# An attention-plus-FFN kernel: attention held to an even rate, shorter output descriptors, wider margins and a new account of DMA times in the scheduler

## Chip, cores, metric

The kernel runs on one core of one Trainium2 chip. The metric is device time in microseconds (us), the median of several executions. Ratios are computed as the mean time of one kernel's fast runs over that of the other kernel's fast runs of the same rounds, so they are not quite the ratio of the medians quoted beside them. Every set of runs has its own runs of the kernel before, made on the same chip.

## The reference, cut to what matters

```python
B, H, S, D = 8, 12, 448, 64            # batch, heads, rows, head size
scores = q @ k^T / 8                    # per head
scores = einsum('bhij,hg->bgij', scores, w_pre)    # heads are mixed before the softmax
attn   = softmax(scores)
attn   = einsum('bhij,hg->bgij', attn, w_post)     # and mixed again after it
x      = (attn @ v), heads side by side # 3584 rows of 768
out    = relu(x @ w_in)**2 @ w_out      # w_in 768x2048, w_out 2048x768, float32 out
```

## The kernel before

The kernel plans its own order. A list scheduler in the program builds one static sequence of instructions for each engine, with a rough account of how long each takes; the order is fixed when the program is built. TensorE has eight streams of units: transposes (T), QK, pre-mix, post-mix, AV, the two halves of the FFN (F1, F2), and a direct form of the first ten pre-mix chunks.

A *chunk* is 10 query rows x 12 heads = 120 partitions; there are 360 chunks. QK scores go from PSUM to an SBUF tile `stage`; a DMA then re-lays each chunk from "one row per partition" to "row and head per partition" (`dring`), so that a matmul can mix heads (pre-mix). ScalarE (ACT) takes the exponential and its row sum, VectorE (DVE) the reciprocal, GpSimd (POOL) folds it into the post-mix weights (`wk2s`), and TensorE mixes again (post-mix).

This is how the scheduler picks the next unit for TensorE:

```python
MARGIN = 250.0
MARGIN_DMA = 3000.0
...
    est = max([t.end + SEM_LAT ... for t in needs ...])     # when the inputs should be there
    safe = est + (MARGIN_DMA if u.dma else MARGIN)          # u.dma: the pre-mix, which needs dring
...
    first = min(f[0] for f in found)
    sure = [f for f in found if f[1] <= first + 1.0]        # those that are ready with the margin
    if sure:
        late = self.ahead()
        def rank(f):
            p = u.prio                                      # post 2, pre 3, QK 4, ... F1 6, F2 7
            if late and u.paced:                            # pre-mix and post-mix are paced
                p += 5.0
            ...
        f = min(sure, key=rank)
    else:
        f = min(found, key=lambda f: (f[0], f[2].prio))     # nothing is sure: the earliest
```

With `ahead()` true, FFN units go before pre-mix and post-mix, if FFN units are ready:

```python
        def ahead():
            done = (f_all[0] - len(s_F1)) / f_all[0] + (f_all[1] - len(s_F2)) / f_all[1]
            return NG - len(s_post) > LEAD + NG * done / 2          # LEAD = 60, NG = 360
```

So before, attention could run up to 60 chunks ahead of the FFN's share of the work. The scheduler also keeps an account of DMA times (a re-layout "move" takes 480 ns of service, more behind loads). The output rows leave like this (`osb` is the SBUF tile that they leave from):

```python
        osb = sb("osb", [128, NOS, F], DT.float32)                  # F = 768
        ...
        dst = bass.AP(out.tensor, row * F, [[RJ * F, m], [1, F]])   # rows of 3072 bytes
        eng.dma_start(dst, osb[p0:p0 + m, s, :]).then_inc(sem_out[s].handle, 16)
```

The softmax here doesn't subtract the row's maximum and nothing guards it: scores larger than these inputs give would overflow.

## Time and profile before

| | before |
|---|---|
| time, median of 3 | 609.08 us (608.08 to 609.39) |
| span of the profiled run | 609.5 us |
| TensorE busy | 582.5 us, 96% |
| mean granted TensorE clock | 0.991 |

The page of the kernel before: busy time of the engines, and TensorE's busy share and granted clock in 40 slices of 15 us, in tenths:

```profile
PE 582.5 (96%) x5998; PEld 391.9 (64%) x5998; DVE 350.3 (57%) x891; ACT 452.2 (74%) x1166; POOL 338.7 (56%) x686
PE   4989999999999899899999999999999999999995
PEclk9989999999999999999899999999999999999998
```

TensorE bounds the kernel: besides the 96%, the page gives it 80% of the chain of work that ended last. But 96% does not say how much is left: in the timeline, 384-column matmuls start every 162 ns, while the page gives 328 ns for one of them. So I measured steps from one matmul's start to the next. For each kind of step I took the usual length, and I call what a step has above it a *wait*, if it is more than 150 ns. (A fixed 0.2 us at the row-tiled QK pairs is left out.) In the profile of before this gives 22.6 us of waits in a stream of 594 us: 7.6 in the first 80 us, 1.5 from 80 to 160, 4.3 from 160 to 240, 6.9 from 240 to 320 and 2.3 afterwards. (The level depends on what is taken as usual. A recount of all the traces, made when this text was checked, takes the median for each pair of successive kinds of matmul, so that the longer step at a change of tiling mode does not count as a wait: in before, a post-mix matmul is followed by the next post-mix after 52 ns, by a QK matmul after 145 (medians). It gives 19.7 us here and 12.4 after the change; sizes differ by a microsecond or a few, and the directions named in this text hold in both counts unless it says otherwise.)

The view of waits of before, TensorE alone (total us, times, longest):

```profile
PE ps L577 <- DMA kraw<-in_k_dram: 8.1, 1, 8.1
PE ps L776 <- DMA dring<-stage: 4.3, 7, 1.0
PE ps L840 <- POOL wk2s L810: 1.6, 3, 0.7
PE ps L701 <- ACT stage L377: 1.3, 3, 0.9
PE ps L840 <- ACT stage L377: 0.9, 3, 0.4
```

The first line is the start (the first load of k), which the orders hardly change: 8.1 to 8.8 us in before, after, e1, e2, e5, e7 and p1. After that, the pre-mix waits for its re-layout (`dring`, 4.3 us), and QK and post-mix for PSUM banks that evictions of scores (`stage`, 1.3 and 0.9 us) hold. The number of pre-mix matmuls in equal stretches of before (the windows view of tile `dring`; the count after x is what to read):

```profile
80.00:160.00 80.00, 19.56 (x60) 7.62 (x60) 1.00 0.82 149
160.00:240.00 80.00, 19.30 (x60) 7.27 (x59) 1.00 0.79 148
240.00:320.00 80.00, 19.43 (x61) 7.80 (x61) 0.98 0.72 131
320.00:400.00 80.00, 11.98 (x45) 5.68 (x45) 1.00 0.54 106
400.00:480.00 80.00, 9.41 (x41) 5.37 (x41) 1.00 0.44 85
```

Attention is done at 60 chunks per 80 us up to 320 us and at 41 to 45 afterwards. The stretch with many chunks is where the waits are.

The timeline of TensorE before, around 292 us (start, length, instructions, and in brackets the idle time ahead of them):

```profile
291.59 0.39 PE L701 MATMUL ps<-qkt 64*88 64x448 bf16 x2
292.83 0.91 PE L701 MATMUL ps<-qkt 64*88 64x448 bf16 x4 [0.86 <-ACT stage L377]
293.88 0.38 PE L840 MATMUL ps<-wk2s,pring 120*128 120x120 bf16 x4
294.10 0.35 PE L776 MATMUL ps<-dring,wk 120*120 120x448 bf16 x1
294.68 0.58 PE L840 MATMUL ps<-wk2s,pring 120*128 120x120 bf16 x4 [0.23 <-ACT stage L377]
295.06 2.77 PE L1043 MATMUL ps<-w_out_sb,h2t 128*128 128x384 bf16 x8
```

After about two microseconds of waits, eight 384-column matmuls take 2.77 us, twice what they take elsewhere (8 x 162 ns = 1.3 us). The record of the granted clock has an interval of 3.413 us at 0.5 from 294.6 us on.

### The profile page before, as it was taken

The page shows a single profiled execution, that of the slowest core. Times are in us where ns is not written, and L with a number is a line of the kernel's source. Part 1 is how long each engine was busy: PE and PEld are TensorE (multiplying, and loading weights), DVE is VectorE, ACT ScalarE, POOL GpSimd, SP SyncE. Part 2 cuts the span into 40 slices and gives each one's busy share as a digit, 9 for nine tenths or more (in the row PEclk, how much of TensorE's full clock was granted, in tenths as well). Part 3 has the DMA queues.
Part 4 walks back from the last instruction along what each step waited for, and adds up shares of the span by engine and source line. Part 5 has one row for each costly group of instructions (what it writes and reads, how often), then busy time and mean ns, then how long its engine had stood idle before and what let it go on. Part 6 is the DMA issues. An engine that isn't in the chain of part 4 may idle for free.

```text
span 609.5 us, 15842 instructions
## 1 busy us (share of the span) xinstructions
PE 582.5 (96%) x5998; PEld 391.9 (64%) x5998; DVE 350.3 (57%) x891; ACT 452.2 (74%) x1166; POOL 338.7 (56%) x686
## 2 busy tenths in 40 slices
PE   4989999999999899899999999999999999999995
PEld 3657776677776556566565666657655765566963
DVE  4777876688778568747674355643544365432410
ACT  1887848888979698889797788787788786665621
POOL 8688586295946366755367543466357444842011
PEclk9989999999999999999899999999999999999998
DMA  9999879686978785768586274525642386311002
GB/s 138 180 225 210 136 125 184 144 147 127 165 134 151 148 176 98 121 111 148 127 152 114 48 153 103 125 47 84 142 102 46 71 151 147 63 21 53 27 29 76
DMA packets 94762, 72.38 MB, mean 119 GB/s; under 512 B 6160, under 2 KB 92640, under 8 KB 94688
## 3 DMA queue, kind: packets, MB, share of 16 engines
q0 software_dynamic: 48992, 33.83, 35.8%
q1 hardware_dynamic: 45696, 37.56, 28.6%
q8 instruction: 48, 0.79, 0.5%
q14 instruction: 26, 0.21, 0.1%
HBM read 45.70 MB, written 11.01 MB: 93 GB/s over the span
## 4 chain that ended last, share of the span: by engine, by line
PE 80%; DMA 8%; ACT 4%; SPq 3%; DVE 2%; POOL 1%; issue 1%; POOLq 0%; ACTq 0%; DVEq 0%
PE ps L1043 23%; PE ps L961 20%; PE ps L840 11%; PE ps L776 10%; DMA dring<-stage 7%; PE ps L902 7%; PE ps L701 6%; PE ps L577 3%; SPq L748 3%; ACT stage L377 2%; DMA kraw<-in_k_dram 1%; ACT pring L794 1%; DVE w_out_sb L621 1%; POOL h2t L999 1%; DVE stage L378 1%
## 5 line engine op out<-in xcount | busy, mean ns | idle before, releaser
L794 ACT ACTIVATE pring<-ps 120x448 bf16<-120x448 f32 x360 | 192.0, 553 | 28.2 <-PE ps L776 26.8
L810 POOL TENSOR_SCALAR wk2s<-wk2b,rinv 120x120 bf16<-120x120 bf16 x350 | 124.9, 364 | 114.1 <-DVE rinv L804 111.5
L961 PE MATMUL ps<-xt,w_in_sb 128*128 128x448 bf16 (+6 forms) x1248 | 171.6, 281 | 1.1 <-issue 0.5
L1043 PE MATMUL ps<-w_out_sb,h2t 128*128 128x384 bf16 x896 | 170.3, 328 | 0.1
L378 DVE CAST a2t<-ps 112x480 bf16<-112x480 f32 x205 | 131.3, 651 | 57.4 <-PE ps L840 55.0
L999 POOL TENSOR_TENSOR h2t<-h1t 128x448 bf16<-128x448 bf16 (+6 forms) x176 | 113.5, 659 | 42.0 <-ACT h1t L989 21.7
L961 PEld LDWEIGHTS ps<-xt,w_in_sb 128*128 128x128 bf16 x1248 | 99.7, 98 | 46.3 <-issue 7.3
L840 PE MATMUL ps<-wk2s,pring 120*128 120x120 bf16 x1440 | 120.8, 217 | 3.5 <-POOL wk2s L810 1.6
L840 PEld LDWEIGHTS ps<-wk2s,pring 120*128 120x128 bf16 x1440 | 94.7, 98 | 44.7 <-issue 5.7
L1043 PEld LDWEIGHTS ps<-w_out_sb,h2t 128*128 128x128 bf16 x896 | 83.9, 98 | 52.9 <-issue 5.0
L378 DVE CAST stage<-ps 120x896 bf16<-120x896 f32 (+2 forms) x87 | 93.6, 1083 | 31.3 <-PE ps L701 20.6
L776 PE MATMUL ps<-dring,wk 120*120 120x448 bf16 x350 | 103.1, 357 | 4.9 <-DMA dring<-stage 4.3
L377 ACT ACTIVATE stage<-ps 120x896 bf16<-120x896 f32 (+3 forms) x99 | 89.1, 917 | 18.3 <-PE ps L701 13.4
L804 DVE RECIPROCAL rinv<-rowsum 120x1 f32<-120x1 f32 x360 | 53.6, 156 | 83.9 <-ACT pring L794 83.0
L377 ACT ACTIVATE a2t<-ps 112x480 bf16<-112x480 f32 x155 | 86.3, 574 | 19.5 <-PE ps L840 17.3
L794 ACT ACTIVATION_READ_ACCUMULATOR pring<-ps 120x1 f32 x360 | 78.2, 217 | 0.0
L1089 POOL DMA_DIRECT2D out_dram<-osb x56 | 30.7, 549 | 68.4 <-ACT osb L377 60.7
L989 ACT ACTIVATE h1t<-ps 128x448 bf16<-128x448 f32 (+5 forms) x105 | 44.6, 429 | 27.7 <-PE ps L961 26.7
L701 PE MATMUL ps<-qkt 64*120 64x448 bf16 (+3 forms) x372 | 58.3, 378 | 2.1 <-ACT stage L377 1.3
L776 PEld LDWEIGHTS ps<-dring,wk 120*120 120x120 bf16 x350 | 44.2, 133 | 21.2 <-DMA dring<-stage 3.7
L990 DVE TENSOR_SCALAR h1t<-ps 128x448 bf16<-128x448 f32 (+6 forms) x103 | 41.6, 407 | 23.4 <-PE ps L961 18.5
L902 PE MATMUL ps<-a2t,vraw 112*64 112x230 bf16 (+5 forms) x864 | 41.1, 255 | 0.0
(37 smaller groups left out, 329.3 us busy)
## 6 DMA issues: line engine op xcount, KB each, us to landing
dring<-stage SPq DMA_DIRECT2D x342, 105.0 KB
vraw<-in_v_dram POOLq DMA_DIRECT2D x24, 224.0 KB, 5.8
qraw<-in_q_dram POOLq DMA_DIRECT2D x23, 224.0 KB, 5.9
kraw<-in_k_dram POOLq DMA_DIRECT2D x23, 224.0 KB, 7.3
w_in_sb<-in_moe_w_in_dram POOLq DMA_DIRECT2D x8, 384.0 KB, 10.4
w_out_sb<-in_moe_w_out_dram POOLq DMA_DIRECT2D x12, 256.0 KB, 33.6
out_dram<-osb POOLq DMA_DIRECT2D x8, 336.0 KB, 3.9
out_dram<-osb POOLq DMA_DIRECT2D x8, 288.0 KB, 3.4
```

Of the source, the lines that this page charges most:

```text
L377: return eng.activation(o, i_, AF.Copy)
L378: return eng.tensor_copy(o, i_)
L701: r_ = eng.matmul(ps[0:nr, banks[par], 0:S], qkt[r0:r0 + 64, pb, p, 0, i0:i1], qkt[r0:r0 + 64, pb, p, 1, :], start=True, stop=True,)
L776: return eng.matmul(ps[0:NR, bank, 0:S], wk1[:, :, :], dring[:, slot, :], start=True, stop=True)
L794: return eng.activation(pring[:, pr, 0:S], ps[0:NR, bank, 0:S], AF.Exp, accum_out=rowsum[:, pr, :])
L804: return eng.reciprocal(rinv[:, pr, :], rowsum[:, pr, :])
L810: return eng.tensor_scalar(wk2s[:, ws, :], wk2b[:, :, :].rearrange("p a b -> p (a b)"), rinv[:, pr, :], 1.0, op0=ALU.mult, op1=ALU.mult)
L840: r_ = eng.matmul(ps[0:128, bank, jb * NR:(jb + 1) * NR], pring[:, pr, jb * JB:jb * JB + 128], wk2s[:, ws, :], start=True, stop=True,)
L902: r_ = eng.matmul(ps[kk * 64:kk * 64 + 64, bank, x * n:(x + 1) * n], vraw[:, h, r, :], a2t[half][:, r, h, a0:a0 + n], start=(r == 0), stop ...
L961: r_ = eng.matmul(ps[:, bank, 0:n], w_in_sb[:, ft, t16 * 128:(t16 + 1) * 128], xt[:, ft, c0:c1], start=(ft == 0), stop=(ft == NFT - 1),)
L999: return eng.tensor_tensor(h2t[:, t16, o0:o0 + n], h1t[:, s, 0:n], h1t[:, s, 0:n], ALU.mult)
L1043: r_ = eng.matmul(ps[:, bank, 0:FH], h2t[:, t16, col:col + 128], w_out_sb[:, t16, hh * FH:(hh + 1) * FH], start=(t16 == 0), stop=(t16 == N ...
```

## The change

Its intent: spread attention evenly, so that neither the re-layout DMA nor the evictions are crowded; put consumers further behind producers; and keep large output packets out of the way of re-layout packets. The diff, cut to its core:

```diff
-MARGIN = 250.0
-MARGIN_DMA = 3000.0
+MARGIN = 500
+MARGIN_DMA = 4000
 ...                                   # the scheduler's account of a move behind loads
-                    at += min(behind, 2600.0)
-                    service += 600.0
+                    at += min(behind, 2000.0)
+                    service += min(behind, 12.0 * max(
+                        [45.0] + [x.dma[2] for x in self.loads if x.end > at]))
 ...
-                t.end = self.move_free + 2100.0
+                t.end = self.move_free + 2200.0
 ...
-        LEAD = 60
+        LEAD = 70
+        PACE = (60000, 30, 1400)
+        OP = F // 4
 ...
-        osb = sb("osb", [128, NOS, F], DT.float32)
+        osb = sb("osb", [128, NOS, 4, OP + 8], DT.float32)
 ...                                   # a move's service 480 -> 620
-                        dst = bass.AP(out.tensor, row * F, [[RJ * F, m], [1, F]])
+                        dst = bass.AP(out.tensor, row * F, [[RJ * F, m], [OP, 4], [1, OP]])
 ...                                   # an output's service n * 350 -> n * 200 + 1000
-            return NG - len(s_post) > LEAD + NG * done / 2
+            made = NG - len(s_post)
+            return made > LEAD + NG * done / 2 or made > PACE[1] + (
+                plan.free[PE] - PACE[0]) / PACE[2]
```

So there are four parts: the *pace* (one chunk per 1.4 us while FFN is ready), the *margins*, the *DMA account* of the scheduler (which the short description of the change does not name) and the *short rows* (768-byte pieces). The first three move only the order of instructions; no matmul is added or removed.

More of the change, by code (lines that the diff above doesn't have):

```diff
@@ L129, in _commit @@
         if t.dma:
-            kind, service = t.dma
+            kind, service, piece = t.dma
             if kind == "load":
@@ L488, in put @@
                                      after=[last.get("load")],
-                                     dma=("load", step * S * D * 4 * LOADR))
+                                     dma=("load", step * S * D * 4 * LOADR, 45.0))
                         last["load"] = t
@@ L514, in put @@
                         -2e5 + VPOS if b == 0 else b * 1000.0 - 1600.0, sem_v, 16,
-                        dma=("load", 4 * S * D * 4 * LOADR)))
+                        dma=("load", 4 * S * D * 4 * LOADR, 45.0)))
                     if len(ts) == 3:
@@ L546, in emit_load_w @@
                         (-2e5 if i == 0 and j == 0 else WPRIO + i) + j * 0.1, sem_w[i][j], 16,
-                        after=[last.get("load")], dma=("load", F * FF // NWP // nx * 4 * LOAD))
+                        after=[last.get("load")], dma=("load", F * FF // NWP // nx * 4 * LOAD, 45.0))
                     last["load"] = t
@@ L752, in emit_rel @@
             t = plan.add("rel%d_%d" % (b, c), SP, fn, sev[(b, T)] + [pre_of.get(g - NDS) if g - NDS >= ND else None],
-                         {SP: (815.0, 0.0)}, g * 1.0, sem_dsl[slot], 16, dma=("move", 480.0))
+                         {SP: (815.0, 0.0)}, g * 1.0, sem_dsl[slot], 16, dma=("move", 620.0, 0.0))
             rel[g] = t
@@ L1064, in fn_oe @@
             def fn_oe(eng, en, hh=hh, bank=bank, s=s):
-                return copy(eng, en, osb[:, s, hh * FH:(hh + 1) * FH], ps[:, bank, 0:FH])
+                return copy(eng, en, osb[:, s, 2 * hh:2 * hh + 2, 0:OP],
+                            ps[:, bank, 0:FH].rearrange("p (a b) -> p a b", a=2))
             t_oe = add("oev%d_%d_%d" % (b, tile, hh), FLEX, fn_oe, [t_o, o_free.get(s)],
@@ L1087, in fn_od @@
                     for p0, m, row in pieces:
-                        dst = bass.AP(out.tensor, row * F, [[RJ * F, m], [1, F]])
-                        eng.dma_start(dst, osb[p0:p0 + m, s, :]).then_inc(
+                        dst = bass.AP(out.tensor, row * F, [[RJ * F, m], [OP, 4], [1, OP]])
+                        eng.dma_start(dst, osb[p0:p0 + m, s, :, 0:OP]).then_inc(
                             sem_out[s].handle, 16)
@@ L1095, in after_F2 @@
                                 {POOL: (580.0 * n, 0.0)}, b * 1000.0 + 710,
-                                sem_out[s], 16 * n, dma=("load", n * 350.0))
+                                sem_out[s], 16 * n, dma=("load", n * 200.0 + 1000.0, 45.0))
                 o_free[s] = t_od
```

## The prediction

> **What bounds the kernel now.** TensorE. The page gives it 582.5 of 609.5 us busy (96%); the chain of waits is 80% PE. I took start-to-start steps from the timeline: 448-column matmuls follow each other every 189 ns, 384-column ones every 162, 120-column ones every 52. All PE instructions at those rates sum to about 560 us. With 8.1 us before the first transpose (wait for kraw) and about 7 us from the last matmul to the end, some 575 us is a floor (estimate from the trace); about 34 us are mode changes beyond that sum, clock dips and waits.

> Waits over 150 ns in the PE stream (without the fixed 0.2 us at each row-tiled QK pair, line 701) add up to only about 20 us: 5 us in the first 40 us, 13 us from 40 to 330, 2 us after. By releaser: DMA dring<-stage about 6 us (8 waits, worst at 193-203 and 245-252 us), evictions of QK scores (stage) about 7, GpSimd's wk2s folds 2, clock dips 1 to 3.

> **What the change does.** (1) The pace rule holds attention at one chunk per 1.4 us while FFN is ready. From the order of instructions: before, chunks come at 17 to 18 per 20 us of PE work from 160 to 280 us, then stop and go; after, 14 to 15 from 120 to 360. (2) Margins 250 to 500 and 3000 to 4000 ns put consumers further behind producers; runs of the pre-mix matmul (line 776) fall from 212 to 141, PE groups from 996 to 893. No matmul is removed; I count 14 more mode changes at about 0.1 us: +1.3 us. ([...] the trace shows 280 instead of 186 ns at such a step.) (3) An output packet of 6144 B takes 239 ns on a DMA engine, one of 3072 B 121, an 896-byte dring packet 54; [...]. With 768 B a dring packet would wait about 50 ns (estimate from 512- and 896-byte packets) instead of up to 239. But outputs are in flight only in 28 short bursts: worth 0 to 2 us. GpSimd issues get dearer: now 541 ns; loads with four pieces per row take about 740, so +0.2 us x 56 = 11 us on an engine 56% busy, and perhaps +0.5 us at the tail.

> **Critical path.** At most the 15 us of waits after 40 us can go; I expect 9 to 10 of them to go, less 1.3 us of mode changes and 0.5 us of tail: about -7.5 us.

> **Prediction:** 601.5 us, 8 in 10 between 596.5 and 608.5. Faster by over 2%: 0.12; same: 0.85; slower: 0.03.

> **What would show it.** PE waits for dring below 2 us; waits for stage evictions halved; PE waits between 160 and 320 us at the level of 330 to 480; output packets of 768 B near 50 ns; output issues near 730 ns; last matmul about 7 us earlier; the same 8 us at the start.

> **What would make it wrong.** New waits where pre-mix matmuls come in batches (ACT needs 770 ns for each exponential), long output landings that hold osb, more half-clock intervals, a gap at the end of the attention; the other way, evictions that unblock more than I count.

## The result

| | before | after |
|---|---|---|
| median | 609.24 us (608.08 to 609.68, 4 runs) | 603.97 us (602.95 to 604.73, 4 runs) |
| ratio of fast runs | | 0.9915 (0.9895 to 0.9936) |
| span, profiled run | 609.5 us | 602.4 us |
| granted clock, profiled run | 0.991 | 0.997 |

The same lines of the page of after:

```profile
PE 579.5 (96%) x5998; PEld 390.1 (65%) x5998; DVE 355.4 (59%) x904; ACT 445.5 (74%) x1153; POOL 341.7 (57%) x686
PE   4988899999999999999999999999999999999995
PEclk9999999999999999999999999999999999999998
```

TensorE's busy share is again 96%: by that number nothing happened. The slices are what changed: from the sixth on there is no 8 left, and the two slices with a lower clock ahead of the last one are gone. The waits of TensorE after (lines of the program have moved by 3):

```profile
PE ps L580 <- DMA kraw<-in_k_dram: 8.4, 1, 8.4
PE ps L843 <- POOL wk2s L813: 2.0, 4, 0.6
PE ps L580 <- issue: 1.0, 1, 1.0
PE ps L779 <- DMA dring<-stage: 0.7, 2, 0.5
PE ps L843 <- DVE h1t L993: 0.5, 1, 0.5
```

The wait for the re-layout fell from 4.3 to 0.7 us. The pre-mix matmuls of after in the same stretches:

```profile
80.00:160.00 80.00, 16.05 (x56) 7.04 (x56) 1.00 0.75 139
160.00:240.00 80.00, 13.96 (x56) 6.93 (x56) 1.00 0.78 144
240.00:320.00 80.00, 13.59 (x55) 6.91 (x55) 1.00 0.68 128
320.00:400.00 80.00, 14.54 (x60) 7.68 (x60) 1.00 0.62 117
400.00:480.00 80.00, 12.75 (x49) 6.13 (x49) 1.00 0.51 99
```

The rate is 55 to 60 up to 400 us, where it was 60 and then 45. By my measure the waits were 22.6 us before and are 16.6 after: 11.2 in the first 80 us (more than the 7.6 of before), 2.6 from 80 to 160, and 2.7 in all the rest, where before had 13.5. From the first to the last matmul, the two profiled runs account as follows:

| | before | after | difference |
|---|---|---|---|
| waits outside half-clock intervals | 21.4 us | 16.6 us | -4.8 |
| lost in half-clock intervals (2, none) | 4.2 us | 0.0 us | -4.2 |
| all else (mode changes 248, 262) | 568.7 us | 570.1 us | +1.4 |
| first to last matmul | 594.3 us | 586.7 us | -7.6 |

The profiled pair differs by more than the medians do (7.1 us of span against 5.3). The profiled run of before was one of the longer of its kind: it took 611.25 us and its clock was 0.991. And of the 4.2 us at most 3.4 can be the clock itself (half of 2 x 3.413 us); the rest is waiting inside the two intervals. In the three sets of experiments below, the runs of before (11 in each) have mean clocks of 0.996, 0.996 and 0.994, while after has 0.997. One 3.413 us interval at half clock costs 0.5 x 3.413 / 608 = 0.0028 of the mean clock, so those runs had on average up to about one such interval more than after (an estimate from these records), and not two. That is why only part of the 4.2 us appears in the medians.

### The profile page after: what moved, and what is told of

Read it like the earlier page. It is cut to its first block, busy times and chain, and to the rows that moved or that the text cites. A ratio compares the mean times of both kernels' runs of the same rounds, so it can differ in the third digit from the quotient of the medians.

```text
span 602.4 us, 15913 instructions
## 1 busy us (share of the span) xinstructions
PE 579.5 (96%) x5998; PEld 390.1 (65%) x5998; DVE 355.4 (59%) x904; ACT 445.5 (74%) x1153; POOL 341.7 (57%) x686
## 4 chain that ended last, share of the span: by engine, by line
PE 89%; DMA 3%; ACT 3%; POOL 2%; SPq 1%; DVE 1%; issue 1%; POOLq 0%
PE ps L1046 25%; PE ps L964 24%; PE ps L843 12%; PE ps L779 10%; PE ps L704 7%; PE ps L905 6%; PE ps L580 4%; DMA dring<-stage 2%; ACT stage L380 1%; SPq L751 1%; DMA kraw<-in_k_dram 1%; POOL h2t L1002 1%; POOL wk2s L813 1%; ACT pring L797 0%; PE ps L653 0%
## 5 line engine op out<-in xcount | busy, mean ns | idle before, releaser
L1046 PE MATMUL ps<-w_out_sb,h2t 128*128 128x384 bf16 x896 | 165.8, 326 | 0.2
L843 PE MATMUL ps<-wk2s,pring 120*128 120x120 bf16 x1440 | 118.0, 216 | 3.3 <-POOL wk2s L813 2.0
L843 PEld LDWEIGHTS ps<-wk2s,pring 120*128 120x128 bf16 x1440 | 92.8, 97 | 43.2 <-issue 7.7
L380 ACT ACTIVATE stage<-ps 120x896 bf16<-120x896 f32 (+3 forms) x104 | 92.9, 919 | 19.2 <-PE ps L704 18.3
L381 DVE CAST stage<-ps 120x896 bf16<-120x896 f32 (+2 forms) x82 | 88.3, 1085 | 19.7 <-PE ps L704 18.8
L779 PE MATMUL ps<-dring,wk 120*120 120x448 bf16 x350 | 90.2, 354 | 1.5 <-DMA dring<-stage 0.7
L1093 POOL DMA_DIRECT2D out_dram<-osb x56 | 35.3, 632 | 76.7 <-ACT osb L380 69.5
L993 DVE TENSOR_SCALAR h1t<-ps 128x448 bf16<-128x448 f32 (+6 forms) x111 | 45.5, 410 | 33.8 <-PE ps L964 28.1
L992 ACT ACTIVATE h1t<-ps 128x448 bf16<-128x448 f32 (+6 forms) x97 | 41.7, 432 | 25.1 <-PE ps L964 23.9
L380 ACT ACTIVATE osb<-ps 128x384 f32<-128x384 f32 x33 | 16.2, 490 | 35.4 <-PE ps L1046 34.9
```

The lines of the kernel that those rows point to most:

```text
L380: return eng.activation(o, i_, AF.Copy)
L381: return eng.tensor_copy(o, i_)
L779: return eng.matmul(ps[0:NR, bank, 0:S], wk1[:, :, :], dring[:, slot, :], start=True, stop=True)
L843: r_ = eng.matmul(ps[0:128, bank, jb * NR:(jb + 1) * NR], pring[:, pr, jb * JB:jb * JB + 128], wk2s[:, ws, :], start=True, stop=True,)
L993: return eng.tensor_scalar(h1t[:, s, 0:n], ps[:, bank, 0:n], 0.0, None, op0=ALU.max)
L1046: r_ = eng.matmul(ps[:, bank, 0:FH], h2t[:, t16, col:col + 128], w_out_sb[:, t16, hh * FH:(hh + 1) * FH], start=(t16 == 0), stop=(t16 == N ...
```

## The experiments

My theory was that the order saves, and that it does so by the pace: fewer chunks per time give the re-layout and the evictions time. The rivals were that the short rows save (re-layout packets pass sooner), that the margins save, or that the DMA account does. Twelve kernels ran, all with five rounds, and all gave correct results.

### The short rows alone, and everything but the short rows

```diff
 # shortened: the copy from PSUM into the padded osb, which goes with it, is left out
 # e1_desc_only: the kernel before with these alone (same order on every engine as before)
+        osb = sb("osb", [128, NOS, 4, OP + 8], DT.float32)
+        dst = bass.AP(out.tensor, row * F, [[RJ * F, m], [OP, 4], [1, OP]])
 # e2_after_long_desc: the kernel after without them (same order on every engine as after)
```

> The kernel before with the 768-byte output rows alone; the order of instructions on every engine is that of before. Schedule theory (the gain comes from the order, the descriptors are worth nothing): 609 us, ratio 1.000 +- 0.002. Descriptor theory (re-layout packets no longer wait behind 6144-byte output packets): about 2 to 5 us less, 604 to 607, and PE waits for dring down by half. Clock theory (each longer PE wait is followed by a 3.4 us interval at half clock, as twice in the before profile, none in the after profile): the clock stays near 0.991 if the waits at 36 and 292 us stay.

> The changed kernel with 3072-byte output rows again; the order of instructions on every engine is that of after. Schedule theory: 604 us, ratio 0.991 to 0.992, clock 0.997, output issues back at 541 ns. Descriptor theory: 606 to 609.

Measured: e1 611.29 us against 609.86 (one of its six runs, 618.54 us at a clock of 0.988, was in the slow state and is not in the ratio), ratio 1.0024 (0.998 to 1.0068). e2 603.83 us, ratio 0.9904 (0.9873 to 0.9935), as good as the whole change. So the short rows are worth nothing that five rounds can show; the gain is in the order. The records of the DMA packets fit this. In before, from rows of 3072 B, output packets have 6144 B (1536 of them, median 239 ns on their DMA engine) or 3072 B (121 ns). In after I had expected 768 B near 50 ns. They have 4608 B (2048 of them, 187 ns), 3072 B (121 ns) or 1536 B (65 ns): six, four or two times the 768 B of a piece, and none has 768 B. By these lengths a re-layout packet that waits for one output packet gains about 50 ns and not 190; that is an estimate from the medians, and that it does wait for one was not shown. The issue on GpSimd did get dearer; the group of before, then that of after:

```profile
L1089 POOL DMA_DIRECT2D out_dram<-osb x56 | 30.7, 549 | 68.4 <-ACT osb L377 60.7 <-DVE rinv L804 5.5 <-issue 1.1
```

```profile
L1093 POOL DMA_DIRECT2D out_dram<-osb x56 | 35.3, 632 | 76.7 <-ACT osb L380 69.5 <-DVE rinv L807 5.9 <-DVE osb L381 0.8
```

That is 549 to 632 ns, 4.6 us in all on an engine that does not bound (busy for 56 and 57% of the span).

e1 also shows how much one order varies between runs. Its order is that of before, and its profile has this in the waits view, where before has 4.3 us:

```profile
PE ps L777 <- DMA dring<-stage: 7.4, 11, 1.3
```

The same goes for the order of after: e2 has it too, and where after has 0.7 us, its profile has

```profile
PE ps L779 <- DMA dring<-stage: 2.4, 5, 0.6
```

Waits for a DMA differ from run to run (e1 and e2 also have the other kind of rows). The fall is in both pairs of profiles, 4.3 to 0.7 and 7.4 to 2.4, but no single figure is firm. The runs of before spread over 606.2 to 612.6 us in this set, those of e2 over 602.7 to 604.2.

### Taking the three scheduler parts apart

```diff
 # in words, not as they stand in the files
 # e5_pace_only, on before:   + PACE = (60000, 30, 1400), LEAD = 70, the new ahead()
 # e3_margins_only, on before: + MARGIN = 500, MARGIN_DMA = 4000
 # e7_model_only, on before:  + the new account of DMA times (short rows not)
 # e8_pace_margins, on before: + pace and margins
 # e4_after_old_margins, on after: - MARGIN = 500, 4000   + 250, 3000
 # e6_after_no_pace, on after:     - PACE, LEAD = 70       + LEAD = 60, the old ahead()
```

> The changed kernel with the old rule of when attention is ahead (LEAD 60, no PACE), everything else as after. If the even pace is what saves: 608 to 610, with PE waits of 13 us or so between 40 and 330 us as before, and dring waits back. If the margins and the cost model save: 603 to 605.

> The changed kernel with the old margins (250 and 3000 ns), everything else as after. If the margins save by putting consumers later: 606 to 609, with more short waits of 0.2 to 0.5 us on stage and dring. If the pace alone saves: 603 to 605, the same waits as after.

> The kernel before with the wider margins alone (500 and 4000 ns). Margin theory: 604 to 606, dring waits below 2 us. Pace theory: 607 to 610. Cost-model theory (the order is only good when the scheduler's account of DMA times is right): 607 to 610.

> The kernel before with the pace rule alone (PACE and LEAD 70), old margins and old DMA account. Pace theory: 604 to 606, and the waits between 160 and 320 us gone while those before 80 us stay. Margin theory: 607 to 610.

> Only the edits to the scheduler's account of DMA times (service 620 for 480 ns, delay behind loads, 200n+1000 for an output), without pace, margins and short rows. Cost-model theory: 604 to 606, dring waits below 2 us. Pace and margin theories: 608 to 610.

> The kernel before with pace and margins, without the new DMA account and the short rows. If the two named edits of the schedule are the whole change: 603 to 605. If the new DMA account matters: 606 to 608 with dring waits of 3 us or more left.

Measured, with the 95% interval. (e4, e6 and after have the short rows, which by e1 and e2 do not matter.) The last three columns are from the profile of each: waits from 80 us on, waits of the pre-mix for `dring` in the whole run, and half-clock intervals of 3.4 us between 50 and 590 us.

| pace | margins | DMA account | kernel | median us | ratio to before | waits after 80 us | dring | half-clock |
|---|---|---|---|---|---|---|---|---|
| - | - | - | before | 609.9, 611.2, 611.4 in three sets | 1 | 15.0 | 5.8 | 1 |
| - | yes | - | e3 | 620.96 | 1.0172 (1.0133 to 1.0211) | 20.4 | 9.1 | 3 |
| - | - | yes | e7 | 624.49 | 1.0239 (1.0189 to 1.029) | 26.3 | 14.9 | 4 |
| - | yes | yes | e6 | 616.94 | 1.0116 (1.0071 to 1.016) | 22.8 | 2.7 | 2 |
| yes | - | - | e5 | 608.42 | 0.997 (0.993 to 1.001) | 12.9 | 1.4 | 0 |
| yes | yes | - | e8 | 610.32 | 1.0009 (0.9964 to 1.0054) | 11.4 | 3.4 | 0 |
| yes | - | yes | e4 | 609.36 | 1.0002 (0.9968 to 1.0037) | 15.2 | 1.2 | 0 |
| yes | yes | yes | after | 603.97 | 0.9915 (0.9895 to 0.9936) | 5.3 | 1.2 | 0 |

No theory that names one part survives as I had put it. Pace alone gives 0.3%, not the whole. Margins alone make it 1.7% slower and the DMA account alone 2.4%. e8 and e4 are no better than before, although each lacks only one part. Yet the pace is ahead in every pair that differs by it alone: 1 against 0.997, 1.0172 against 1.0009, 1.0239 against 1.0002, 1.0116 against 0.9915. The first of these differences is within the noise (the interval of e5 reaches 1.001); the other three are not. In the profiles the last column splits the same way: no half-clock interval after 50 us in the orders with the pace, one to four in those without it. But that is one profile of each kernel. The mean clock of all fast runs, which includes the time before 50 us, is 0.996 for e5, for e8 and for before in the same set, so between these three the split does not show; it shows for e3 (0.992), e6 (0.990) and e7 (0.982). In the recount of waits, e5, e8 and e4 have less from 80 us on than before (9.0, 7.8 and 10.6 us against 12.4) and still no shorter time beyond the noise: the waits after 80 us alone do not set the time. The extreme is e7, whose waits view and clock line of the page read:

```profile
PE ps L779 <- DMA dring<-stage: 11.7, 16, 1.4
```

```profile
PEclk9999999997999999999799999999999999999998
```

### Is the order a draw?

That every single edit of the scheduler other than the pace made before slower was suspicious. A list scheduler is chaotic: a small edit gives another order. If before had been tuned until a good order came out, then any edit loses that order, and the loss is put down to the edit. So I nudged both kernels by values that mean nothing.

```diff
 # n2_before_margin260:  - MARGIN = 250.0   + MARGIN = 260.0
 # n1_after_margin520:   - MARGIN = 500     + MARGIN = 520
```

> The kernel before with MARGIN 260 instead of 250, again a nudge without meaning. If before was itself tuned to a lucky draw (which would explain that single edits to it cost 1.7 and 2.4%): 612 to 625. If its rules are worth 610: 607 to 613.

> The changed kernel with MARGIN 520 instead of 500, a nudge that has no meaning of its own but gives another order (PE groups 900 instead of 893). If the gain belongs to the rules: 602 to 606. If the order is a draw of which the changed kernel got a good one: anywhere from 602 to 612.

Measured: n2 619.18 us against 611.36, ratio 1.0124 (1.0077 to 1.0172); one of its six runs, the profiled one, 626.23 us at a clock of 0.983, was in the slow state and is not in the ratio. n1 605.17 us, ratio 0.9916 (0.9876 to 0.9955). So ten nanoseconds of margin cost before 1.2%, and twenty cost after nothing. The order of before looks like a lucky one of its rules; that of after did not prove so under the one nudge that it was given. Over the five orders without pace (before, n2, e3, e7, e6) the mean ratio is (1 + 1.0124 + 1.0172 + 1.0239 + 1.0116) / 5 = 1.013, and before is the best of them. Over the six with pace (e5, e8, e4, after, n1, and v1 below) it is (0.997 + 1.0009 + 1.0002 + 0.9915 + 0.9916 + 0.9931) / 6 = 0.996. By that estimate the pace is worth about 1.7%; the four pairs above, alike in the other scheduler parts, give 1.6% on average. Most of it does not show when before and after are compared, because before is 1.3% better than the mean of its five. It stays an estimate: each order is one draw, and the orders of a group differ in the other parts too.

What this leaves open: whether margins and DMA account are worth the 0.9% by which e8 and e4 trail after. Each of them is one order, and the order of one kernel moved by 1.2% under a nudge. Two good neighbours (after and n1) speak for it; they do not settle it.

### The early waits of after

After has more waits in its first 80 us than before. The pace line allows 16 chunks at 40 us, 30 at 60 and 44 at 80. In the trace of after, 18, 28 and 45 post-mixes have started by then, so the rule is at its limit in this stretch and may be what makes the waits.

```diff
 # v1_early_off, on after
-            return made > LEAD + NG * done / 2 or made > PACE[1] + (
-                plan.free[PE] - PACE[0]) / PACE[2]
+            return made > LEAD + NG * done / 2 or (
+                plan.free[PE] > 80000 and made > PACE[1] + (plan.free[PE] - PACE[0]) / PACE[2])
```

> The changed kernel with the pace rule off for the first 80 us, where the changed kernel has 11.2 us of PE waits against 7.6 before. If the rule causes those early waits: about 8 us of them and 600 to 602 us. If the early waits come with the latency of the first chunks whatever the rule: 603 to 607.

Measured: 606.37 us, ratio 0.9931 (0.9893 to 0.9969). I had expected 600 to 602 us if the rule causes the early waits. The early waits did fall, to 7.0 us (one profile), so the rule does seem to cause 4 us of them; but those from 80 to 160 us rose from 2.6 to 6.6 and the sum is 20.0 against 16.6. That the chunks which are not held back early are crowded a little later is my reading of this; it was not tested. As an improvement this fails, and no version that I ran beats after by more than the noise.

### What a wait costs

```diff
 # p1_five_stalls, on after, when the order is made (shortened, partly in words)
+        for at in (150e3, 220e3, 290e3, 360e3, 430e3):
+            x = <the first F1 task on TensorE that ends after `at`>; y = <the next one on TensorE>
+            <SP: once x is done, load 128 x 12 values to a scratch tile>; y waits for that load
```

> The changed kernel with TensorE made to wait five times, at about 150, 220, 290, 360 and 430 us, for a small load issued when the instruction before was done. Each wait should be 2.5 to 3.5 us. If waits only cost themselves: 604 + 5 x 3 = about 619 us and a clock of 0.997. If a wait of 2 us or more within one 3.41 us interval brings an interval at half clock: some of the five also show one, the clock falls to 0.985 or so, and each costs about 1.7 us more: 622 to 628.

Measured: 637.5 us, ratio 1.0424 (1.0378 to 1.047), clock 0.97 in the profiled run. I had expected waits of 3 us; two were longer (4.9 and 9.9): there the small load was issued late, behind re-layouts on its queue, and in the longer one it also took 8.1 us to land, beside loads of q and k. The sum of the five idle times is 2.8 + 9.9 + 4.9 + 2.6 + 3.0 = 23.2 us, but the profiled span grew by 638.9 - 602.4 = 36.5 us. The rest, 13.3 us, goes with ten half-clock intervals of 3.413 us. (Half of their time is 17 us, but in some of it TensorE was waiting anyway.) Each of the five waits has one or more of them, from 160.4, 238.9, 320.8, 402.8 and 477.9 us on, starting within the wait or right after it, and after 50 us there are no others; the one at 37.5 us was not made by them and followed other waits. The profile of after has none. The first of the five in the timeline:

```profile
158.12 0.45 PE L964 MATMUL ps<-xt,w_in_sb 128*128 128x218 bf16 x3
161.35 0.63 PE L704 MATMUL ps<-qkt 64*120 64x448 bf16 x2 [2.77 <-DMA scratch<-in_w_pre_dram]
161.91 0.73 PE L964 MATMUL ps<-xt,w_in_sb 128*128 128x218 bf16 x3
162.43 2.45 PE L779 MATMUL ps<-dring,wk 120*120 120x448 bf16 x6
```

After 2.77 us of idle time, six pre-mix matmuls take 2.45 us, where at full clock one starts every 189 ns. And its page:

```profile
PEclk9989999999799997999979999899999999999998
```

So each of these five waits, of 2.6 to 9.9 us, brought the half clock, and not the reverse; for shorter waits in pieces only the correlation is shown. In an ordinary run a smaller share of the gain of after comes this way than in the profiled pair, as said above: the clock of before was 0.994 to 0.996 on average, and 0.997 in after.

## Why the prediction was right

The time was 603.97 us, inside 596.5 to 608.5, and "same" (within 2%) was the class with 0.85. Point by point:

- **"TensorE is nearly dense; at most 15 us of waits after 40 us can go."** Right, and it is what kept the forecast small. Waits from 80 us on fell from 15.0 to 5.3 us.
- **"I expect 9 to 10 of them to go."** The sum came out, its parts did not, and that they add up is luck. In the profile, waits outside half-clock intervals fell by 4.8 us and half-clock loss by 4.2. From 80 us on the waits did fall by 9.7 us, but 3.6 us came back as early waits, which I had not foreseen. I had sized "clock dips" at 1 to 3 us and did not connect them with waits; p1 shows that they followed from its five long ones (2.6 to 9.9 us).
- **"+1.3 us of mode changes."** 248 became 262, as counted from the order. All other time of the stream grew by 1.4 us; it was not tested by itself.
- **"About -7.5 us."** The profiled pair has -7.1, the medians -5.3. The size was off because the profile that I read was of a run with two half-clock intervals, more than the average run of before has.
- **"PE waits for dring below 2 us."** Right in the profile of after: 5.8 to 1.2 us by my measure, 4.3 to 0.7 in the waits view. The same order in e2 has 2.4 us there.
- **"Waits for stage evictions halved."** Nearly: about 7 to 4 us by my measure; in the waits view 3.9 to 1.0.
- **"Waits between 160 and 320 us at the level of 330 to 480."** Right: 11.2 us became 1.1; 320 to 480 us has 1.6.
- **"With 768 B a dring packet would wait about 50 ns."** Wrong. The pieces have 768 B, but most of the packets have 4608 B and take 187 ns. That a re-layout packet waits for one output packet was my assumption; it was not shown. I had given this 0 to 2 us, and e1 and e2 show no gain.
- **"Output issues near 730 ns", "+0.5 us at the tail."** 632 ns; from the last matmul's start to the end it took 7.1 us before and 7.3 after.
- **"Last matmul about 7 us earlier; the same 8 us at the start."** 602.4 to 595.1 us; 8.1 and 8.4.

What the prediction did not see at all is that the kernel before seems to have a lucky order. It took before's waits as what its rules give; one nudge gave 1.2% more time.

## What to carry to other kernels

When a scheduler makes the order, compare rules over several orders: nudge a constant that should not matter in both versions, and see whether one version falls apart. On a TensorE that is almost full, spread the work that needs other engines evenly, because here waits that added up to 1.87 us or more within one 3.413 us interval were mostly followed by half clock (ten times, against seven intervals that were not followed by my measure and one in the recount). And read the packets, not the descriptors, before you shorten transfers to let others pass: here pieces of 768 B went out in packets of 1536 to 4608 B.
